# A delta-rule attention with a feed-forward layer: block 1's masks, joins and weight splits in another order

## The chip, the cores and the metric

The kernel runs on one core of one Trainium2 chip. The metric is the device time of one execution in microseconds (us). Before the change the median of three runs is 632.37 us (632.14 to 633.58).

## The reference

Inputs: q, k, v of shape (4, 8, 768, 48) (batch, heads, steps, width) and beta (4, 8, 768); weights w_in (384 x 2048) and w_out (2048 x 384), all float32. For every batch and head, one step after the other:

```
kn = k / (|k| + 1e-6);  state = 0                     (48 x 48)
for t in 768 steps:
    y[t]   = q[t] @ state
    state += beta[t] * outer(kn[t], v[t] - kn[t] @ state)
x = y as (3072 tokens, 384)
h = x @ w_in;  out = max(0.01 * h, h) @ w_out
```

## The kernel before

**Blocks.** The 768 steps are cut into 12 blocks of 64 (`nblk`). Within a block the recurrence becomes a triangular system; only its result and the state pass to the next block. Each block has a Gram product (`gram`: k with k and q), an inverse (`inv`), the attention (`solve`) and the feed-forward layer of its 256 tokens (`ffn`, 16 slices f of 128 hidden units). `gram` masks its product with the triangle on VectorE (`masked`, L320: rq), copies k's part with ScalarE (L307: gs) and the corners with VectorE (L328: gm), and writes gs through DRAM (L311: gd) into L, the system in the layout of the inverse (L341). Blocks 0 and 1 get their Gram from `first` instead (masks at L264) and are inverted together (b = 0); every later block alone. b counts the inverses: L1 and T1 belong to block 2, L2 and T2 to block 3.

**Inverse and attention.** `inv` takes the norms from L's diagonal (`norms`, L360 to L369, sixteen short steps on VectorE up to L423) and then runs 31 elimination steps (`eliminate`, L384 and L389, two interleaved chains). For a single block T is then copied by ScalarE in another layout (L449), and both layouts go through DRAM (td at L456, tt at L457). For blocks 0 and 1, `place` copies the halves of T to their places (L468). `merge_z` and `merge_u` join the halves (pz, pu; from block 2 on pz needs the transfers sq from tt and td, L516 and L519). `solve` then goes through stages kt (pk, and beta on VectorE, L623), step_w (pw), step_y (py) and step_s (pc); `columns` (px) makes x of the next block.

**The layer.** For block 0 it runs in float32, for the others as three products of high and low halves (fp32r): x is split in xh and xl, the hidden activation in gh (ScalarE, L722) and gl (VectorE, L727). The weights come in eight packed groups j of two f. Per group: load_w (a DMA), `pack` (ScalarE, L148), `conv` (four steps on VectorE, L158 to L161), `expand` (ScalarE, L168), `final` (VectorE, L175), after which block 0 can use it; `lows` then makes the halves for block 1 on (ScalarE casts the high part, L184; VectorE subtracts, L186). `pack` of group j uses the buffer of group j - 5, so packs 5, 6 and 7 wait for lows 0, 1 and 2.

**The order.** All generators are written in one program order: every block has 17 slots, slot s starts with slice s of `ffn`, then come the entries of the table `work` for that slot, then steps of `solve`, `inv` and `gram`, spread over the slots of `SV`, `IV` and `GG`. `behind(mark)` adds that an instruction isn't issued before a marked one. From this a scheduler fixes the order of each engine's queue when the kernel is built; on the chip each engine works its queue in that order. SP issues nearly all DMAs. PSUM leaves four buffers (`ps_a`) in rotation for all products but the layer's.

Of the kernel before, what the change touches and what calls it, by code (L numbers as in the profile page):

```python
# [47 lines left out]
def delta_moe_kernel(ctx: ExitStack, tc, kq0, kqT, kv, qT, beta, cst, w_all, out, nblk):  # L48
# [66 lines left out]
    wi, wo = ([{}, {}] for _ in range(2))  # L115
    raws, mark = {}, {}

    def behind(name):

        return tc.issue_after(mark[name]) if name in mark else nullcontext()  # L120

# [57 lines left out]
    def lows(j, gate):  # L179
        g = parts[j][0]  # L180
        t = sb.tile([P, 8 * DO], F32R, tag=f"w{j}", name=f"w{j}", bufs=1)
        hi, lo = t[:, 0:4 * DO], t[:, 4 * DO:]
        with behind(gate):
            nc.scalar.copy(hi, g)  # L184
# [16 lines left out]
    def first():  # L201
# [28 lines left out]
        for g in range(NGR):  # L230
            for i, y, u, (k, _) in each(g):
                l = (g * GU + u) * HC
                for e in range(2):
                    h = k[:, e * HC:(e + 1) * HC]
                    nc.tensor.matmul(diag[y][i * 64 + e * HC:i * 64 + (e + 1) * HC, l:l + HC], h, h, start=True, stop=True)
# [9 lines left out]
        for g in range(NGR):  # L245
            for i, y, u, (k, _) in each(g):
                l = (g * GU + u) * HC
                nc.tensor.matmul(low[y][corner[i], l:l + HC], k[:, HC:], k[:, 0:HC], start=True, stop=True)
# [6 lines left out]
        for g in range(NGR):  # L255
            for i, y, u, (k, q) in each(g):
                nc.tensor.matmul(bank[g][y][i * 64:(i + 1) * 64, u * C:(u + 1) * C], k, q, start=True, stop=True)
        yield
        for n in range(2):
            for g in range(NGR):  # L260
# [6 lines left out]
            after(d)  # L267
            done.add((gram, n))
# [4 lines left out]
    def gram(n):  # L273
# [16 lines left out]
        for g in range(NGR):  # L290
# [7 lines left out]
            for p in range(NPAIR):  # L298
                for c in range(2):
                    for b in range(2):  # L300
                        r = slice(b * R0, b * R0 + D)
                        with behind("ph") if n > 2 else nullcontext():
                            nc.tensor.matmul(ps[b][c * 64:(c + 1) * 64, p * 128:(p + 1) * 128],  # L303
# [70 lines left out]
    def eliminate(b, L, j, T, m):  # L374
# [4 lines left out]
        for x in range(min(m, 2)):  # L379
# [19 lines left out]
    def inv(b):
# [28 lines left out]
        for j in range(HC - 1):  # L428
# [3 lines left out]
            if j == HC - 2:  # L432
# [13 lines left out]
                else:  # L446
                    n = NB[b][0]
                    Tt = X[:, M * HC:].rearrange("p (i m) -> p i m", m=M)
                    nc.scalar.copy(Tt.rearrange("p i m -> p m i"), T)  # L449
                    td = dr.tile([2, HC, HS, HC], F32, tag="td", name=f"td{n}")  # L450
                    tt = dr.tile([HS, HC, HC], F32, tag="tt", name=f"tt{n}")
                    Tts[n] = td, tt
                    for x in range(2):
                        a = x * 64
                        for e in range(2):
                            nc.sync.dma_start(td[e, x::2].rearrange("m l i -> l m i"), T[a + e * HS:a + (e + 1) * HS])  # L456
                        nc.sync.dma_start(tt.rearrange("l i (x m) -> x l i m", m=M)[x], Tt[a:a + HS])  # L457
# [8 lines left out]
    def place(n, g, e):  # L466
        a = n * 64 + e * HC
        with behind("h" if n else "inverse"):  # L468
            return (nc.scalar.copy if e or n else nc.vector.tensor_copy)(
                half_of(n, g, e), Tts[n][0][a:a + HC].rearrange("p (y g u) i -> p g y u i", y=2, g=NGR)[:, g])  # L470
# [10 lines left out]
    def product(n, name, pairs):  # L481

        ps = ps_a.tile([P, 512], F32, tag="a", name=f"{name}{n}")
        with behind("po"):
            for q, w, lhs, rhs in pairs:
                nc.tensor.matmul(ps[q * HC:(q + 1) * HC, w * P:(w + 1) * P], lhs, rhs, start=True, stop=True)  # L486
        return ps[:, 0:2 * P]

    def merge_z(n, g, t):

        T, Tt = Tts[n]
        if n < 2:
# [34 lines left out]
    def merge_u(n, g, t):  # L527

        if n < 2:
# [32 lines left out]
    def lengths(n):  # L562
# [3 lines left out]
        nc.tensor.matmul(ps[DN, 0:HS], nrm[b][i * 64:i * 64 + 64], eye0[i * 64:i * 64 + 64], start=True, stop=True)  # L566
# [13 lines left out]

    def solve(n):
# [5 lines left out]
        nt = nts.pop(n)  # L587
# [21 lines left out]
        def kt(g):  # L609

            t, k, v = tv(n, g), of("k", n, g), of("v", n, g)
            if n:
                pv = out_of("pk", g, C)
                for c, u, r in heads(D):
                    nc.tensor.matmul(pv[r, u], k[DN, c, u], t[DN, c, u // NPAIR, u % NPAIR], start=True, stop=True)  # L615
                for c in range(2):
                    nc.scalar.mul(t[UP, c], pv[c * 64:c * 64 + D].rearrange("p (y v) t -> p y v t", y=2), -1.0)  # L617
            if not n:
                return
            for s in range(GS):  # L620
                us = slice(s * NPAIR, (s + 1) * NPAIR)
                with behind("gl"):
                    nc.vector.tensor_tensor(  # L623
                        v[DN, :, us], v[DN, :, us],
                        nt[DN, g, :, us].rearrange("p h (u o) -> p h u o", o=1).broadcast_to([C, 2, NPAIR, D]), ALU.mult)

        def step_w(g):
            t, v = tv(n, g), of("v", n, g)
            pv = out_of("pw", g, D)
            for c, u, e in quarters():  # L630
                a = c * C + e * HC
                nc.tensor.matmul(pv[a:a + HC, u], t[:, c, u // NPAIR, u % NPAIR, e * HC:(e + 1) * HC], v[:, c, u], start=True, stop=True)  # L632
# [276 lines left out]
```

## Time and profile before

| | |
|---|---|
| median of 3 runs | 632.37 us |
| profiled execution | 629.7 us, its span 627.9 us |
| TensorE (PE), its weight loads (PEld) | busy 582.0 us (93%), 533.5 us (85%) |
| VectorE (DVE) | busy 432.8 us (69%) |
| ScalarE (ACT) | busy 329.9 us (53%) |
| chain of work that ended last | PE 81%, DVE 7%, ACT 5%, DMA 3% |

The profile is of one execution. A busy share is a mean over the whole span, in which the first three blocks differ from the rest: the weights are converted there, and the first inverses run. What is read of a single block is read from its own stretch of the trace. A stretch is named by the first gh of a block; there the layer's slice 0 of that block begins.

### The profile page before, as it was taken

What the parts mean: (1) busy time and instruction counts of PE and PEld (TensorE: products, weight loads), DVE (VectorE), ACT (ScalarE), POOL (GpSimd) and SP (SyncE); (2) the same over time, 40 slices, a digit from 0 to 9 for tenths busy, and PEclk for the clock granted to TensorE, in tenths of its full rate; (3) what the DMA queues carried; (4) which work ended last, traced back from release to release, by engine and by line L of the source; (5) the groups of instructions that cost most, each with busy time, mean ns of one, the idle gap of its engine ahead of it and who ended that gap; (6) DMA issues with size and microseconds to landing.
All of it is one profiled execution on the core that took longest, in us unless ns stands there. A gap on an engine that the chain in (4) does not pass through costs nothing.

```text
span 627.9 us, 22383 instructions
## 1 busy us (share of the span) xinstructions
PE 582.0 (93%) x9122; PEld 533.5 (85%) x9122; DVE 432.8 (69%) x1949; ACT 329.9 (53%) x818; POOL 10.7 (2%) x17
## 2 busy tenths in 40 slices
PE   5278899979989989999999999999999999999996
PEld 4266677869978989999999999999999989999996
DVE  3999889979747959659659669669669569221212
ACT  3477975656535355545545545555545545544432
POOL 6000000000000000000000000000000000000000
PEclk9989999989999999999999999999999999999999
DMA  5986923361364650461560570561460540500101
GB/s 123 319 251 235 285 63 79 69 98 25 67 129 97 142 91 9 101 136 30 105 149 14 106 158 13 99 150 33 89 151 22 96 99 4 98 14 3 25 2 26
DMA packets 123431, 59.69 MB, mean 95 GB/s; under 512 B 111296, under 2 KB 114496, under 8 KB 122304
## 3 DMA queue, kind: packets, MB, share of 16 engines
q1 hardware_dynamic: 120576, 57.27, 40.0%
q10 hardware_dynamic: 2752, 0.98, 0.8%
q8 instruction: 72, 1.18, 0.8%
q14 instruction: 31, 0.25, 0.1%
HBM read 46.96 MB, written 11.27 MB: 93 GB/s over the span
## 4 chain that ended last, share of the span: by engine, by line
PE 81%; DVE 7%; ACT 5%; DMA 3%; issue 2%; SPq 1%; DVEq 0%; ACTq 0%
PE ph L719 32%; PE po L709 31%; PE pk L615 3%; PE pw L632 3%; PE py L652 3%; PE pc L642 3%; DVE T L389 2%; DVE tmp L384 2%; PE pg L303 2%; ACT gh L722 1%; PE px L687 1%; PE pu L486 1%; PE pz L486 1%; DMA kx<-in_kq 1%; DMA gd<-gs 1%
## 5 line engine op out<-in xcount | busy, mean ns | idle before, releaser
L719 PE MATMUL ph<-xh,w 128*128 128x256 f32 x1056 | 224.7, 289 | 0.0
L719 PEld LDWEIGHTS ph<-xh,w 128*128 128x128 f32 x1056 | 174.8, 189 | 7.1 <-issue 2.0
L727 DVE TENSOR_TENSOR gl<-ph,gh 128x256 fp32r<-128x256 f32 x176 | 74.4, 423 | 154.0 <-ACT ph L726 152.1
L709 PE MATMUL po<-w,gh 128*128 128x384 f32 x704 | 172.8, 343 | 5.4 <-ACT gh L722 5.4
L722 ACT ACTIVATE gh<-ph 128x256 fp32r<-128x256 f32 (+1 forms) x192 | 73.7, 384 | 158.1 <-PE ph L719 152.2
L719 PE MATMUL ph<-xl,w 128*128 128x256 f32 x528 | 149.0, 284 | 0.0
L709 PEld LDWEIGHTS po<-w,gh 128*128 128x128 f32 x704 | 121.0, 188 | 9.9 <-ACT gh L722 7.9
L389 DVE TENSOR_TENSOR T<-T,tmp 128x60 f32<-128x60 f32 (+35 forms) x661 | 111.8, 207 | 0.8
L384 DVE TENSOR_TENSOR tmp<-T,L 128x60 f32<-128x60 f32 (+35 forms) x661 | 111.2, 207 | 0.8
L709 PE MATMUL po<-w,gl 128*128 128x384 f32 x352 | 106.2, 338 | 0.0
L719 PEld LDWEIGHTS ph<-xl,w 128*128 128x128 f32 x528 | 99.9, 189 | 1.3 <-issue 0.4
L726 ACT ACTIVATE ph<-ph 128x256 f32<-128x256 f32 x176 | 67.2, 382 | 0.0
L709 PEld LDWEIGHTS po<-w,gl 128*128 128x128 f32 x352 | 61.3, 188 | 0.1
L617 ACT ACTIVATE rt<-pk 48x512 f32<-48x512 f32 x44 | 26.0, 592 | 22.4 <-PE pk L615 21.6
L320 DVE TENSOR_TENSOR rq<-pg,csb 64x256 f32<-64x256 f32 x80 | 33.9, 423 | 3.8 <-ACT gs L307 2.5
L634 ACT COPY rv<-pw 64x384 f32<-64x384 f32 x48 | 22.7, 473 | 13.4 <-PE pw L632 12.5
L644 ACT COPY rv<-pc 48x384 f32<-48x384 f32 x44 | 20.9, 475 | 11.9 <-PE pc L642 11.4
L719 PE MATMUL ph<-x,cg 128*128 128x256 f32 x96 | 24.5, 393 | 2.0 <-DVE cg L175 1.2
L719 PEld LDWEIGHTS ph<-x,cg 128*128 128x128 f32 x96 | 18.4, 197 | 7.8 <-DVE cg L175 1.6
L709 PE MATMUL po<-cg,gh 128*128 128x384 f32 x64 | 24.5, 503 | 0.0
L303 PE MATMUL pg<-kq 48*64 48x128 f32 x640 | 23.3, 274 | 0.0
L652 PEld LDWEIGHTS py<-rv,rq 128*32 128x32 f32 x1536 | 18.3, 112 | 5.5 <-ACT ph L726 2.6
(98 smaller groups left out, 584.9 us busy)
## 6 DMA issues: line engine op xcount, KB each, us to landing
wr<-in_w_all SPq DMA_DIRECT2D x8, 1536.0 KB, 13.1
kq<-in_kqT SPq DMA_DIRECT2D x40, 192.0 KB, 3.9
L<-gd SPq DMA_DIRECT2D x20, 256.0 KB, 4.0
rk<-in_kv SPq DMA_DIRECT2D x24, 192.0 KB, 3.4
rv<-in_kv SPq DMA_DIRECT2D x24, 192.0 KB, 4.1
rq<-in_qT SPq DMA_DIRECT2D x24, 192.0 KB, 3.7
out<-ob SPq DMA_DIRECT2D x46, 96.0 KB, 2.6
td<-T SPq DMA_DIRECT2D x40, 64.0 KB, 2.6
```

The source lines that it names most:

```text
L303: nc.tensor.matmul(ps[b][c * 64:(c + 1) * 64, p * 128:(p + 1) * 128], kq[r, c ^ b, p, 0], kq[r, c ^ b, p].rearrange("p x t -> p (x t)"), s ...
L320: nc.vector.tensor_tensor(qa[DN, c, b * NPAIR:(b + 1) * NPAIR], pv[b][r, 1], tri[r].rearrange("p (o t) -> p o t", o=1).broadcast_to([C, NP ...
L384: nc.vector.tensor_tensor(tv, t[:, :, j:j + 1].broadcast_to([P, k, w]), L[:, j, j + 1:].rearrange("p (o w) -> p o w", o=1).broadcast_to([P ...
L389: mark["steps"] = nc.vector.tensor_tensor(t, t, tv, ALU.subtract).ins
L617: nc.scalar.mul(t[UP, c], pv[c * 64:c * 64 + D].rearrange("p (y v) t -> p y v t", y=2), -1.0)
L634: d = nc.scalar.copy(v[DN, c], pv[c * 64:c * 64 + C])
L652: nc.tensor.matmul(pv[a:a + HC, u * D:(u + 1) * D], qa[:, c, u, e * HC:(e + 1) * HC], v[:, c, u], start=True, stop=True)
L709: i = nc.tensor.matmul(po[t][:, :DO], a[:, ts_], w, start=(f == 0 and k == 0), stop=(f == NFC - 1 and k + 1 == len(ways)))
L719: i = nc.tensor.matmul(ph, w[:, cc * P:(cc + 1) * P], a, start=(k == 0), stop=(k + 1 == len(ways)))
L722: i = nc.scalar.activation(gh, ph, AF.Prelu, alpha=0.01)
L726: i = nc.scalar.activation(ph, ph, AF.Prelu, alpha=0.01)
L727: mark["gl"] = nc.vector.tensor_tensor(gl, ph, gh.bitcast(F32), ALU.subtract).ins
```

## The change

1. The masks of block 1 go in reversed order of the two head groups, one group ahead of conv(1) and one behind final(0); conv(1) stands ahead of expand(0) and final(0).
2. `place` for block 1 uses eight DMAs on SP in place of four copies by ScalarE.
3. `lows` is split into `cast` (ScalarE) and `lows` (VectorE). The casts of groups 3 to 7 move into block 0's last slots. low(3) comes behind a mark at elimination step 20 (`el1`), lows 4 to 7 behind `el2`, which with two interleaved chains is the last step of one of them.
4. T's copy (blocks 2 to 4) goes to VectorE. td and tt leave in the order td, tt, tt, td, tied by the mark `bounce`; L of block 3 comes behind it.
5. In block 1, slots 0 to 14, `multiply` ties every TensorE instruction to the one written before it.
6. The Gram of block 4 moves from block 2 into block 1's last slots (`GG`); its gd goes by SP, before by ScalarE's queue.
7. `SV` names the slot of each step of `solve`; `IV` and `work` are new tables; the scaling by beta becomes `times` with the same instructions.

```diff
+    def multiply(*args, fn=nc.tensor.matmul, **kw):
+        with behind("pe" if fixed else None):
+            i = fn(*args, **kw)
+        mark["pe"] = i.ins
+        return i
...
-    def lows(j, gate):
+    def cast(j, gate):
...
+        with behind(gate):
+            nc.scalar.copy(t[:, 0:4 * DO], parts[j][0])
...
+    def lows(j):
...
-        with behind("dv"), behind("el2" if j > 2 else None):
+        with behind("dv"), behind("el2" if j > 3 else "el1" if j > 2 else None):
             after(nc.vector.tensor_tensor(lo, g, hi.bitcast(F32), ALU.subtract))
...
-            for g in range(NGR):
+            for g in range(NGR)[::1 - 2 * n]:
...
-                    (nc.scalar if n == GS * NGR else nc.sync).dma_start(
+                    nc.sync.dma_start(
...
-                    i = nc.sync.dma_start(Lh[b0][r * 64:(r + 1) * 64].rearrange("l j i -> l (j i)"), gd.rearrange("l j i -> l (j i)"))
+                    with behind("bounce" if n == 3 else None):
+                        i = nc.sync.dma_start(Lh[b0][r * 64:(r + 1) * 64].rearrange("l j i -> l (j i)"), gd.rearrange("l j i -> l (j i)"))
...
+        if b == 1 and j == 20:
+            mark["el1"] = mark["steps"]
...
-                    nc.scalar.copy(Tt.rearrange("p i m -> p m i"), T)
+                    (nc.vector.tensor_copy if n < 5 else nc.scalar.copy)(Tt.rearrange("p i m -> p m i"), T)
...
+                    rows(0)
                     for x in range(2):
...
+                        with behind("bounce"):
+                            d = nc.sync.dma_start(tt.rearrange("l i (x m) -> x l i m", m=M)[x], Tt[x * 64:x * 64 + HS])
+                        mark["bounce"] = d.ins
+                    rows(1)
...
+        if n:
+            for y in range(2):
+                nc.sync.dma_start(d[:, y], t[:, y])
+            return
...
+    conv(1)
     lo, hi = slice(0, 1), slice(1, 2)
     expand(0, "rv", lo)
     final(0, lo)
-    conv(1)
+    weave(1, (sv, 2, 0, 1))
+    next(gg)
+    for g in range(NGR):
+        for e in (1, 0):
+            place(1, g, e)
+    final(0, hi)
...
+    next(fg)
+    expand(1, "xh")
+    pack(3, "xh")
+    final(1)
+    conv(2)
...
-        4: ((load_w, 7, "dv"), (conv, 4), (final, 3), (lows, 0, "h0_4")),
-        5: ((expand, 4, "h0_5"), (pack, 5, "h0_4")),
-        6: ((conv, 5), (final, 4), (lows, 1, "h0_6")),
-        7: ((expand, 5, "h0_7"), (pack, 6, "h0_6")),
...
-        NF + 0: ((lows, 3, "h1_0"),), NF + 1: ((lows, 4, "h1_1"),),
-        NF + 2: ((lows, 5, "h1_2"),), NF + 3: ((lows, 6, "h1_3"),), NF + 5: ((lows, 7, "h1_5"),)}
+        4: ((pack, 5, "h0_4"), (expand, 4, "h0_4")),
+        5: ((conv, 5), (final, 4), (cast, 1, "h0_5"), (lows, 1)),
+        6: ((pack, 6, "h0_6"), (expand, 5, "h0_6")),
...
+        13: ((cast, 3, "h0_12"),), 14: ((cast, 4, "h0_13"),), 15: ((cast, 5, "h0_14"),), 16: ((cast, 6, "h0_15"), (cast, 7, "h0_15")),
+        NF + 0: ((lows, 3), (lows, 4)), NF + 2: ((lows, 5),), NF + 3: ((lows, 6),), NF + 5: ((lows, 7),)}
...
+            fixed[:] = [True] * (n == 1 and s < 15)
...
-IV, GG = ((9, 17), (6, 17), (6, 17), (2, 17)), ((2, 4), (1, 2), (1, 2))
-SV = (0, 10), (3, 13), (1, 11), (2, 12)
+IV, GG = ((7, 17), (5, 16), (3, 12), (2, 17)), ((2, 6), (1, 2), (12, 13), (16, 17))
+SV = (1, 2, 4, 5, 7, 8, 9), (7, 9, 11, 13, 14, 15), (4, 6, 7, 9, 11, 12), (3, 5, 6, 8, 10, 11)
```

What the scheduler makes of it is seen in the order of each engine's queue (line, operation, output <- inputs, partitions x elements). First VectorE where block 0 goes over into block 1 (w: lows of a group; T1, tmp1: elimination steps for block 2; gl1_0: the first gl of block 1; rq2: masks of block 3's Gram). Before:

```order
L389 TENSOR_TENSOR T1_1483<-T1_1483,tmp1_30_1_1765 128x8
L727 TENSOR_TENSOR gl1_0_1791<-ph0_72,gh1_0_1789 128x256
L384 TENSOR_TENSOR tmp1_29_0_1757<-T1_1483,L1_1072 128x16
L389 TENSOR_TENSOR T1_1483<-T1_1483,tmp1_29_0_1757 128x8x2
L384 TENSOR_TENSOR tmp1_30_0_1763<-T1_1483,L1_1072 128x8
L389 TENSOR_TENSOR T1_1483<-T1_1483,tmp1_30_0_1763 128x8
L186 TENSOR_TENSOR w3_1794<-cg3_966,w3_1794 128x1536
L727 TENSOR_TENSOR gl1_1_1808<-ph1_73,gh1_1_1806 128x256
L186 TENSOR_TENSOR w4_1811<-cg4_1022,w4_1811 128x1536
L320 TENSOR_TENSOR rq2_80<-pg3_0_0_1828,csb_74 64x256 x2
L320 TENSOR_TENSOR rq2_80<-pg3_0_1_1829,csb_74 64x256 x2
```

and now:

```order
L197 TENSOR_TENSOR w5_1703<-cg5_1136,w5_1703 128x1536
L398 TENSOR_TENSOR tmp1_29_0_1771<-T1_1359,L1_1095 128x16
L197 TENSOR_TENSOR w6_1755<-cg6_1274,w6_1755 128x1536
L197 TENSOR_TENSOR w7_1757<-cg7_1397,w7_1757 128x1536
L756 TENSOR_TENSOR gl1_0_1805<-ph0_72,gh1_0_1803 128x256
L756 TENSOR_TENSOR gl1_1_1821<-ph1_73,gh1_1_1819 128x256
L333 TENSOR_TENSOR rq2_80<-pg3_0_0_1838,csb_74 64x256 x2
L405 TENSOR_TENSOR T1_1359<-T1_1359,tmp1_29_0_1771 128x8x2
L333 TENSOR_TENSOR rq2_80<-pg3_0_1_1839,csb_74 64x256 x2
L398 TENSOR_TENSOR tmp1_30_0_1777<-T1_1359,L1_1095 128x8
L405 TENSOR_TENSOR T1_1359<-T1_1359,tmp1_30_0_1777 128x8
L465 COPY T1_1359<-T1_1359 128x16x32
```

The low of group 4 stands one row above the second fence. The lows of groups 4 to 7 now stand ahead of gl1_0; before, lows 3 to 7 came behind it, in turn with the later gl. The last steps of the elimination and T's copy now come behind gl1_1.

Second SP in block 1 (td2 and tt2: the two layouts of T for block 2; gd3 and L2: the Gram of block 3 on its way; sq0 and sq1 feed pz2; kq4: inputs of block 4's Gram). Before:

```order
L456 DMA td2_1770<-T1_1483 32x16x32 x4
L281 DMA kq4_0_2736<-in_kqT 48x1024 x2
L457 DMA tt2_1771<-T1_1483 1024x1x16 x2
L311 DMA gd3_1821<-gs3_0_1826 32x8x32 x4
L516 DMA sq0_1957<-tt2_1771 32x8x32 x4
L311 DMA gd3_1821<-gs3_1_1856 32x8x32 x4
L519 DMA sq1_1959<-td2_1770 32x8x32 x2
L341 DMA L2_1820<-gd3_1821 64x1024 x2
```

and now:

```order
L294 DMA kq4_0_2710<-in_kqT 48x1024 x2
L324 DMA gd3_1831<-gs3_0_1836 32x8x32 x4
L294 DMA kq4_1_2713<-in_kqT 48x1024 x2
L324 DMA gd3_1831<-gs3_1_1866 32x8x32 x4
L473 DMA td2_1784<-T1_1359 32x16x32 x2
L479 DMA tt2_1785<-T1_1359 1024x1x16 x2
L473 DMA td2_1784<-T1_1359 32x16x32 x2
L355 DMA L2_1830<-gd3_1831 64x1024 x2
L541 DMA sq0_2067<-tt2_1785 32x8x32 x4
```

All of gd3 now goes ahead of td2 and tt2, L2 directly behind them, and the sq behind L2.

Third ScalarE in block 0, around the copies gs2_1 of block 2's Gram (rt: copies from pu and pk, cg: pack and expand of a weight group, gh0: hidden activations). Before:

```order
L168 CAST cg4_1022<-cg4_1022 128x1536
L307 COPY gs2_1_1114<-pg2_1_0_1115 128x256
L307 COPY gs2_1_1114<-pg2_1_1_1116 128x256
L540 ACTIVATE rt0_82<-pu1_0_1165 32x2x4x32 x2
L540 ACTIVATE rt1_83<-pu1_1_1184 32x2x4x32 x2
L722 ACTIVATE gh0_6_1258<-ph0_72 128x256
L184 CAST w1_1267<-cg1_409 128x1536
```

and now:

```order
L751 ACTIVATE gh0_5_1180<-ph1_73 128x256
L190 CAST w1_1189<-cg1_409 128x1536
L751 ACTIVATE gh0_6_1270<-ph0_72 128x256
L176 CAST cg5_1136<-cg5_1136 128x1536
L156 COPY cg6_1274<-wr6_982 128x1536
L652 ACTIVATE rt0_82<-pk1_0_1192 48x2x256 x2
L652 ACTIVATE rt1_83<-pk1_1_1213 48x2x256 x2
L320 COPY gs2_1_1234<-pg2_1_0_1235 128x256
L320 COPY gs2_1_1234<-pg2_1_1_1236 128x256
```

The copies gs2_1 stood ahead of the copies from pu and of the cast of group 1; now they stand behind that cast, expand(5), pack(6) and the copies from pk.

## Rows read from the trace of the kernel before

**Rows 1.** Stretches; us, PE, PEld, DVE, ACT, POOL busy (x), PEclk, DMA share, GB/s

```profile
46.90:56.60 9.70, 7.09 (x200) 5.85 (x190) 8.87 (x16) 5.79 (x11) 0.00 (x0) 0.87 0.36 106
117.80:170.40 52.60, 49.25 (x730) 45.14 (x729) 44.21 (x195) 33.46 (x72) 0.00 (x0) 0.97 0.38 69
...
225.10:271.70 46.60, 46.30 (x730) 43.34 (x728) 33.63 (x172) 24.12 (x64) 0.00 (x0) 1.00 0.33 63
```

**Rows 2.** Waits of TensorE, 56 to 240 us: us in total, times, longest

```profile
PE pu L538 <- DVE rq L320: 2.8, 1, 2.8
PE pz L486 <- DMA sq<-tt: 2.3, 1, 2.3
```

**Rows 3.** Timeline of VectorE: start us, us, instruction, count [idle before <-releaser]

```profile
63.92 0.56 DVE L158 TENSOR_SCALAR cg<-cg 128x768 uint32<-128x768 uint32 x1 [0.76 <-ACT cg L148]
...
68.36 1.76 DVE L175 SCALAR_TENSOR_TENSOR cg<-wr,cg 128x1536 uint32<-128x1536 uint32 x1 [1.70 <-ACT cg L168]
...
71.82 1.97 DVE L623 TENSOR_TENSOR rv<-rv,nt 64x384 f32<-64x384 f32 x4
...
80.66 1.75 DVE L320 TENSOR_TENSOR rq<-pg,csb 64x256 f32<-64x256 f32 x4
82.44 0.59 DVE L328 COPY gm<-gs 32x256 f32<-32x256 f32 x2
83.06 1.76 DVE L186 TENSOR_TENSOR w<-cg,w 128x1536 fp32r<-128x1536 f32 x1
86.88 0.56 DVE L158 TENSOR_SCALAR cg<-cg 128x768 uint32<-128x768 uint32 x1 [2.06 <-ACT cg L148]
...
93.01 0.48 DVE L411 MEMSET T<- 128x512 f32 x1
...
119.22 0.42 DVE L727 TENSOR_TENSOR gl<-ph,gh 128x256 fp32r<-128x256 f32 x1
...
144.58 0.35 DVE L363 RECIPROCAL rc<-sr 128x32 f32<-128x32 f32 x1
144.96 0.22 DVE L364 SCALAR_TENSOR_TENSOR rc<-rc,L 128x32 f32<-128x32 f32 x1
...
147.22 1.29 DVE L423 TENSOR_TENSOR L<-L,cb 128x512 f32<-128x512 f32 x2
```

**Rows 4.** Timeline of ScalarE, 75 to 123 us

```profile
75.62 0.67 ACT L307 COPY gs<-pg 128x256 f32<-128x256 f32 x2
...
85.25 1.60 ACT L148 COPY cg<-wr 128x1536 bf16<-128x1536 bf16 x1
86.70 2.44 ACT L617 ACTIVATE rt<-pk 48x512 f32<-48x512 f32 x4
...
121.96 1.12 ACT L449 COPY T<-T 128x512 f32<-128x512 f32 x1
```

**Rows 5.** Timeline of SP (issue of transfers), 80 to 136 us

```profile
80.57 1.83 SPq L311 DMA_DIRECT2D gd<-gs  x4
83.85 1.10 SPq L341 DMA_DIRECT2D L<-gd  x2
...
123.69 1.37 SPq L457 DMA_DIRECT2D tt<-T  x2
...
135.07 1.13 SPq L341 DMA_DIRECT2D L<-gd  x2
```

**Rows 6.** DMA issues of the page: count, KB each, us to landing

```profile
L<-gd SPq DMA_DIRECT2D x20, 256.0 KB, 4.0
```

**Rows 7.** Timeline of TensorE in block 1, start of two f in a row

```profile
135.92 0.28 PE L719 MATMUL ph<-xh,w 128*128 128x256 f32 x1
...
138.04 0.28 PE L719 MATMUL ph<-xh,w 128*128 128x256 f32 x1
```

**Rows 8.** Stretches again, for TensorE's granted clock (PEclk)

```profile
76.80:80.20 3.40, 3.40 (x29) 2.46 (x26) 3.32 (x4) 1.25 (x4) 0.00 (x0) 0.50 0.46 125
219.00:223.00 4.00, 1.77 (x11) 1.45 (x10) 2.08 (x10) 1.99 (x5) 0.00 (x0) 1.00 0.59 130
```

More of the change, by code (lines that the diff above doesn't have):

```diff
@@ L115, in delta_moe_kernel @@
     wi, wo = ([{}, {}] for _ in range(2))
+    fixed = []
     raws, mark = {}, {}
@@ L247, in first @@
                 l = (g * GU + u) * HC
-                nc.tensor.matmul(low[y][corner[i], l:l + HC], k[:, HC:], k[:, 0:HC], start=True, stop=True)
+                multiply(low[y][corner[i], l:l + HC], k[:, HC:], k[:, 0:HC], start=True, stop=True)
             for n in range(2):
@@ L266, in first @@
                           tri[r].rearrange("p (o v t) -> p o v t", o=1, v=1).broadcast_to([C, 2, NPAIR, C]), ALU.mult)
-            after(d)
-            done.add((gram, n))
+                after(d)
+                done.add((gram, n))
+                if n:
+                    yield
             yield
@@ L452, in inv, with rows @@
                     Tts[n] = td, tt
+                    def rows(x):
+                        for e in range(2):
+                            a = x * 64 + e * HS
+                            with behind("bounce"):
+                                d = nc.sync.dma_start(td[e, x::2].rearrange("m l i -> l m i"), T[a:a + HS])
+                            mark["bounce"] = d.ins
+                    rows(0)
                     for x in range(2):
[L454 to L457, printed above, removed]
+                        with behind("bounce"):
+                            d = nc.sync.dma_start(tt.rearrange("l i (x m) -> x l i m", m=M)[x], Tt[x * 64:x * 64 + HS])
+                        mark["bounce"] = d.ins
+                    rows(1)
                 done.add((inv, b))
@@ L467, in place @@
         a = n * 64 + e * HC
-        with behind("h" if n else "inverse"):
-            return (nc.scalar.copy if e or n else nc.vector.tensor_copy)(
-                half_of(n, g, e), Tts[n][0][a:a + HC].rearrange("p (y g u) i -> p g y u i", y=2, g=NGR)[:, g])
+        d, t = half_of(n, g, e), Tts[n][0][a:a + HC].rearrange("p (y g u) i -> p g y u i", y=2, g=NGR)[:, g]
+        if n:
+            for y in range(2):
+                nc.sync.dma_start(d[:, y], t[:, y])
+            return
+        with behind("inverse"):
+            return (nc.scalar.copy if e else nc.vector.tensor_copy)(d, t)
     squares = {}
@@ L579, in lengths, with times @@
                         nc.scalar.mul(v[DN, c, u], v[DN, c, u], nt[DN, g, c, u:u + 1])
+    def times(n, g, nt):
+        v = of("v", n, g)
+        for s in range(GS):
+            us = slice(s * NPAIR, (s + 1) * NPAIR)
+            with behind("gl"):
+                nc.vector.tensor_tensor(
+                    v[DN, :, us], v[DN, :, us],
+                    nt[DN, g, :, us].rearrange("p h (u o) -> p h u o", o=1).broadcast_to([C, 2, NPAIR, D]), ALU.mult)
     def solve(n):
@@ L614, in kt @@
                 for c, u, r in heads(D):
-                    nc.tensor.matmul(pv[r, u], k[DN, c, u], t[DN, c, u // NPAIR, u % NPAIR], start=True, stop=True)
+                    multiply(pv[r, u], k[DN, c, u], t[DN, c, u // NPAIR, u % NPAIR], start=True, stop=True)
                 for c in range(2):
                     nc.scalar.mul(t[UP, c], pv[c * 64:c * 64 + D].rearrange("p (y v) t -> p y v t", y=2), -1.0)
[L618 to L625, printed above, removed]
+            if n:
+                times(n, g, nt)
         def step_w(g):
@@ L641, in step_s @@
                 with nullcontext() if n else behind("ph"):
[L642 removed]
+                    multiply(pv[r, u], k[:, c, u], v[:, c, u], start=True, stop=True)
             for c in range(2):
@@ L832, in delta_moe_kernel @@
                 fn(*args)
-            weave_at(s, n, (sv, (NS + (n == 0)) * (n + 1 < nblk), *SV[at]), (iv, NI * (n + 2 < nblk), *IV[at]),
-                     (gg, NGR * (n < 3), *GG[min(n, 2)]), (gg, NGR * (1 < n < nblk - 3), 12, 13))
+            for k in range(0 if n + 1 == nblk else SV[at].count(s)):
+                next(sv)
+            weave_at(s, n, (iv, NI * (n + 2 < nblk), *IV[at]),
+                     (gg, NGR * (n < 2), *GG[n > 0]), (gg, NGR * (0 < n < nblk - 3), *GG[2 if n > 1 else 3]))
 WEARLY, NPACK, NG = 4, 3, 5
```

64 lines of the change are left out of this document (28 added, 36 removed).

## The prediction

> **What bounds the kernel now.** I read the stretches between the first hidden activations (gh) of the blocks first [rows 1]. Block 3, from 225.1 us to 271.7, takes 46.60 us, and TensorE is busy for 46.30 of them; the later blocks repeat it. Nothing but less work on TensorE could shorten those. Block 1 takes 52.60 us, and block 2, from 170.4 to 225.1, takes 54.7. Together that is 14.1 us more than two such blocks; part of it is the second Gram product that block 2 holds. All of the change lies ahead of block 3. From there on both orders differ in little but SP's, so I leave the rest as it is. The sum asks one thing: when does block 3 start?
>
> Then the waits of TensorE [rows 2]. It waits 2.8 us for VectorE's masks at pu in block 0 and 2.3 us for a transfer at pz in block 1: these two the change attacks by name. The last view is VectorE's order of time in block 0 [rows 3]. It runs almost without a break up to gl1_0, the first gl of block 1, which ends at 119.22 + 0.42 = 119.64. Three waits are left in it: 0.76 at 63.92, 1.70 at 68.36 and 2.06 us at 86.88, all for ScalarE's packs and expands. Block 1 can't begin its second layer before gl1_0. So the wait at pu is not what sets its start: VectorE is. VectorE up to gl1_0 is the first leg of my sum, TensorE in block 1 the second, block 2 the third.
>
> **Leg 1: VectorE up to gl1_0.** Removed: the three waits, 4.52 us. conv(1) and the masks now stand where VectorE waited, and ScalarE loses the four placements that stood ahead of the expands. Added: five lows (subtractions that split the weights). Before, lows 3 to 7 stand behind gl1_0, one between each two gl, where TensorE has work beside them. Now all five stand ahead of it: 5 x 1.76 = 8.8 us [rows 3], four of them in one run just before it, as the order shows. TensorE can't send block 1's products before that, however early it is itself.
>
> One new wait stands on this leg. The second half of block 2's Gram is copied (gs2_1) behind pack(6) and four copies of pk. pack(6) writes a buffer that low(1) must have read. low(1) ended at 83.06 + 1.76 = 84.82; less the first two waits (2.46), and less beta's products, one set of masks and the corner copies, which now follow it (1.97 + 1.75 + 0.59), that is 78.05. A pack takes 1.60, the pk copies 2.44, the two gs copies 0.67 [rows 4]: gs2_1 is there at 82.8. Before, the first gd transfer was issued at 80.57, the second half of L half of 1.10 us behind 83.85 [rows 5], and L takes 4.0 to land [rows 6]: 7.8 us. So L lands at 90.6. VectorE would be there at 93.01 - 4.52 + 0.48 = 89.0 [rows 3], and waits **1.6 us**. The bounds are 0 (pack(6) in time) and 4.4 (the pk copies held for another 2.8 us, as TensorE was at pu). So gl1_0 ends at 119.64 - 4.52 + 8.8 + 1.6 = **125.5**, bounds 123.9 and 128.3.
>
> The eight transfers that now place block 1's halves of T I cost at nothing. They leave SP behind conv(1), when the DMA engines are busy for 0.36 of the time [rows 1]; eight issues at 0.46 (four take 1.83 [rows 5]) and one landing like L's make 7.7 us, and their user, pz1, stands behind block 0's first products, 9.7 us later. If that cover goes, TensorE stands at pz1, and makes it up while it waits for VectorE later. The wait at pu I cost at nothing too: TensorE gets ahead by 2.8 us and waits the longer for gl1_0.
>
> **Leg 2: block 1 from gl1_0.** TensorE's steady 46.30 us hold what is left of the block, except the first products of f1 and f2, which are done by then. One f takes 138.04 - 135.92 = 2.12 us, half of it in its first layer [rows 7]: 46.3 - 2.1 = 44.2. Block 3's Gram is done as well, block 4's comes in: one for one, no gain in this block.
>
> The waits of this leg are those that a fixed order of TensorE can't fill with other work. The L of block 3 (L2) is now issued behind all transfers of T, and these behind T's copy. What the copy costs on VectorE no row shows. The nearest row of the engine is a low, 1.76 us for 1536 elements, a third of which is 0.6; ScalarE's own copy took 1.12 [rows 4]. I take 0.7, near the low, since the engine is the same. It ends at 125.5 + 0.42 + 1.75 (masks) + 0.7 = 128.4. Behind it SP issues tt (1.37), two td (0.9) and half of L2's 1.13 [rows 5]: the last leaves at 131.2 and lands, with 4.0, at 135.2. The six norm steps in front of gl1_5 are two reciprocals at 0.35 and four steps of about 0.2 [rows 3], 1.5 in all; gl1_5 ends at 137.1. TensorE is there at 125.5 + 5 x 2.12 = 136.1: it waits 1.0. The next ten steps take 147.22 + 1.29 - 144.96, less one gl, 3.1 us [rows 3]; gl1_6 ends at 140.6 and TensorE is there at 137.1 + 2.12 = 139.2: 1.4. At the block's end solve's last step now stands in the last slots with little behind it to fill: between 0 and one f (2.1), I take 1.0. Together 3.4, less the 0.3 that a steady block has: block 2 starts at 125.5 + 44.2 + 3.1 = **172.8**. The bounds of these waits are 0 and 12 (the late L2, below). pz2 doesn't wait any longer, it stands behind f5.
>
> **The clock.** After its wait at pu TensorE ran 3.4 us, from 76.8 to 80.2, at 0.50, the lower of its two levels, 1.2 GHz; from 219 to 223, where it stood idle for 2.2 of 4 us, it kept 1.00, 2.4 GHz [rows 8]. The wait for gl1_0, some 8 us by my sum, is of the first kind. I add nothing for it: a stretch of 3.4 us at half speed costs 1.7, and up to gl1_6 TensorE has 2.4 us of waits that take it up. The Trainium skill (TensorE: Matmul & The Clock Gate, section "HAM oscillation — how this bites in real kernels") speaks against this change: there each wait for data throttles the engine anew and the next piece of work starts cold. By that rule every new wait would be paid a second time; that is the cold rival below.
>
> **Leg 3: block 2** has one Gram now and solve(3) spread as in the steady blocks: 46.60 [rows 1]. Block 3 starts at 172.8 + 46.6 = **219.4** against 225.1: 5.7 us less. The profiled execution took 629.7 us, so 624.0; the median, 632.37, stands 2.7 above it, and I forecast **626.7 us**, 0.9% less.
>
> **Rivals.** *Covered waits* (22%): pack(6), L1 and L2 come in time, and the 1.6 of leg 1 and the 3.1 of leg 2 fall away: **622.0**. For it: each is under 2 us. Against it: the queues put the users right behind their sources.
>
> *Late L2, slower* (15%): before, L2 landed at 135.07 + 0.57 + 4.0 = 139.6 [rows 5, 6], 16.5 us after T's copy had ended at 121.96 + 1.12 = 123.08 [rows 4]; I give it 6.8 here. If T's transfers hold it as long as then, gl1_5 comes 9.7 us later, and TensorE, tied to its order, has nothing else to run: **636.4**. It is slower than before by over 0.2% from an L2 landing at 142.1 on. Against it: before, the transfers of the Gram (gd3) and of sq were issued between; now gd3 goes ahead and sq behind.
>
> *Cold TensorE* (18%): the waits for gl1_0 and gl1_5 leave a stretch of 3.4 us at half speed each, and none of it is taken up: 2 x 1.7 = 3.4, **630.1**. The page's rule would make this the likeliest; the row at 219 speaks against it.
>
> That the change does not do what it says is no rival here: the lows in front of gl1_0 and T's transfers in front of L2 stand in the order itself. The forecast keeps 45%.
>
> **The numbers.** 0.2% is 1.3 us, about what a measurement of this kernel can tell from no change. Faster by more (below 631.1): the forecast, the covered waits and somewhat over half of the cold case, 0.77. Slower (above 633.6): most of the late L2, 0.12. Between: 0.11. The range, 620.0 to 634.0, takes in the covered case, with 2 us below it for one f more that TensorE may have done before gl1_0, and the cold one; it stops short of the late L2.
>
> **What would show it.** Right: gl1_0 ending between 124 and 128 with four lows in a run before it and TensorE idle for some 8 us there; no wait at pu in block 0 and none at pz2; VectorE idle once near 89, before the norms of block 2, and once at 132 to 136; block 2 at 46 to 47 us. Wrong: gl1_0 before 122 (the lows cost less than I say) or after 130; TensorE standing at pz1; a granted clock of 0.50 behind 130; L2 landing after 140.

## The result

The changed kernel takes 639.12 us (median of 4 runs, 637.71 to 640.71) against 632.87 for the kernel before: ratio 1.010, 95% interval 1.0071 to 1.0128, 1% slower. The forecast was 626.7, 0.9% faster. The profiled execution took 640.71, the slowest of the four and 1.6 above their median, and its span is 638.9 us against 627.9.

The page shows that the chain that ended last now runs more over VectorE and the transfers (before: PE 81%, DVE 7%, DMA 3%):

```profile
span 638.9 us, 22400 instructions
PE 589.5 (92%) x9122; PEld 538.6 (84%) x9122; DVE 434.5 (68%) x1952; ACT 324.9 (51%) x811; POOL 10.7 (2%) x17
...
PE 77%; DVE 13%; DMA 4%; ACT 3%; issue 2%; SPq 1%; DVEq 0%; ACTq 0%
```

The stretches of the changed kernel, columns as in [rows 1]: block 1, block 1 from gl1_0 on, block 2, block 3:

```profile
122.20:180.10 57.90, 52.06 (x799) 48.38 (x798) 43.70 (x186) 25.71 (x70) 0.00 (x0) 0.94 0.37 66
129.30:180.10 50.80, 49.00 (x724) 45.70 (x725) 36.60 (x180) 21.94 (x60) 0.00 (x0) 0.95 0.33 56
180.10:236.20 56.10, 49.96 (x734) 46.33 (x732) 37.05 (x181) 23.25 (x63) 0.00 (x0) 0.94 0.48 89
236.20:282.60 46.40, 46.10 (x730) 43.17 (x728) 33.80 (x172) 24.19 (x65) 0.00 (x0) 1.00 0.51 103
```

Block 3 starts at 236.2, before at 225.1: all the loss lies ahead of it, as was forecast, but with the other sign. Block 1 takes 57.9 (before 52.6), block 2 56.1 (54.7). Of TensorE's waits from 110 to 240 us 12.0 us are for gl; the one at pz of [rows 2] is gone, and so is the one at pu (none of it between 50 and 110 us):

```profile
PE ph L126 <- DVE gl L756: 12.0, 4, 6.1
PE po L126 <- ACT gh L751: 3.0, 2, 2.7
```

The 2.7 us stand at 117.5, at the end of block 0, where the last gh stands in ScalarE's queue behind an instruction that waits 4.4 us for low(3) on VectorE; gl1_0, which comes later, covers them.

VectorE's timeline shows the waits of leg 1 (1.70, 1.60 and 3.02 us), the lows in front of gl1_0 (at 128.87), T's copy, and two waits for L:

```profile
55.73 1.76 DVE L183 SCALAR_TENSOR_TENSOR cg<-wr,cg 128x1536 uint32<-128x1536 uint32 x1 [1.70 <-ACT cg L176]
...
64.40 1.76 DVE L183 SCALAR_TENSOR_TENSOR cg<-wr,cg 128x1536 uint32<-128x1536 uint32 x1 [1.60 <-ACT cg L176]
...
94.93 0.19 DVE L374 TENSOR_SCALAR sr<-L 128x32 uint32<-128x32 uint32 x1 [3.02 <-DMA L<-gd]
...
122.11 3.42 DVE L197 TENSOR_TENSOR w<-cg,w 128x1536 fp32r<-128x1536 f32 x2
125.44 0.17 DVE L398 TENSOR_TENSOR tmp<-T,L 128x16 f32<-128x16 f32 x1
125.53 3.42 DVE L197 TENSOR_TENSOR w<-cg,w 128x1536 fp32r<-128x1536 f32 x2
128.87 0.75 DVE L756 TENSOR_TENSOR gl<-ph,gh 128x256 fp32r<-128x256 f32 x2
...
132.05 0.62 DVE L465 COPY T<-T 128x512 f32<-128x512 f32 x1
...
141.67 0.19 DVE L374 TENSOR_SCALAR sr<-L 128x32 uint32<-128x32 uint32 x1 [3.12 <-DMA L<-gd]
...
195.58 0.19 DVE L374 TENSOR_SCALAR sr<-L 128x32 uint32<-128x32 uint32 x1 [9.09 <-DMA L<-gd]
```

The last row is the largest: VectorE stands 9.1 us for L of block 4, and gl2_4 queues behind (the expectations below call it gl2_5; counted from gl2_0 at 180.76 it is the fifth, and TensorE waits for it until 197.0). In the kernel before, L of block 4 landed later still, 18.0 us into the block against 15.4, but there seven gl stood ahead of the norms, not four, and VectorE did not wait (SP's timeline, then VectorE's, of the kernel before):

```profile
182.55 1.14 SPq L341 DMA_DIRECT2D L<-gd  x2
```

```profile
191.17 0.12 DVE L360 TENSOR_SCALAR sr<-L 128x32 uint32<-128x32 uint32 x1
```

SP's timeline, where rows 5 had L alone, shows why L is not there by the new place of the norms. From 174.8 to 191.8 it issues almost without a break (the longest, 0.7 us, is ahead of L, for gd to land), and L comes behind sq, out, rt and its own gd:

```profile
174.78 1.78 SPq L541 DMA_DIRECT2D sq<-tt  x4
...
181.83 2.45 SPq L783 DMA_DIRECT2D out<-ob  x4
184.32 0.58 SPq L550 DMA_DIRECT2D rt<-td  x1
185.01 1.95 SPq L324 DMA_DIRECT2D gd<-gs  x4
187.00 0.45 SPq L550 DMA_DIRECT2D rt<-td  x1
187.55 1.92 SPq L324 DMA_DIRECT2D gd<-gs  x4
189.51 0.45 SPq L550 DMA_DIRECT2D rt<-td  x1
190.67 1.13 SPq L355 DMA_DIRECT2D L<-gd  x2
```

The granted clock (PEclk, the third column from the end) was 0.50 behind both of TensorE's long waits, 4.1 us at gl1_0 and 6.1 at gl2_4:

```profile
130.00:134.00 4.00, 4.00 (x18) 4.00 (x18) 3.74 (x11) 0.66 (x2) 0.00 (x0) 0.50 0.62 91
...
198.00:202.00 4.00, 4.00 (x30) 3.15 (x29) 3.87 (x19) 2.14 (x7) 0.00 (x0) 0.50 1.08 172
```

### The profile page after: what moved, and what is told of

It reads as the page before. It is cut to its first block, busy times and chain, and to the rows that moved or that the text cites. A ratio compares the mean times of both kernels' runs of the same rounds, so it can differ in the third digit from the quotient of the medians.

```text
span 638.9 us, 22400 instructions
## 1 busy us (share of the span) xinstructions
PE 589.5 (92%) x9122; PEld 538.6 (84%) x9122; DVE 434.5 (68%) x1952; ACT 324.9 (51%) x811; POOL 10.7 (2%) x17
## 4 chain that ended last, share of the span: by engine, by line
PE 77%; DVE 13%; DMA 4%; ACT 3%; issue 2%; SPq 1%; DVEq 0%; ACTq 0%
PE ph L126 31%; PE po L126 28%; PE pk L126 3%; PE pw L126 3%; DVE T L405 3%; DVE tmp L398 3%; PE pg L126 3%; PE py L126 3%; PE pc L126 2%; DMA L<-gd 2%; DVE w L197 2%; PE pu L126 1%; PE px L126 1%; PE pz L126 1%; DMA kx<-in_kq 1%
## 5 line engine op out<-in xcount | busy, mean ns | idle before, releaser
L126 PE MATMUL ph<-xh,w 128*128 128x256 f32 x1056 | 227.2, 291 | 12.0 <-DVE gl L756 12.0
L126 PEld LDWEIGHTS ph<-xh,w 128*128 128x128 f32 x1056 | 176.7, 191 | 20.0 <-DVE gl L756 13.3
L126 PE MATMUL po<-w,gl 128*128 128x384 f32 x352 | 107.6, 339 | 0.0
L126 PE MATMUL ph<-x,cg 128*128 128x256 f32 x96 | 26.9, 423 | 2.0 <-ACT gh L751 1.6
L612 DVE TENSOR_TENSOR rv<-rv,nt 64x384 f32<-64x384 f32 x44 | 22.4, 555 | 0.6
```

The costliest lines, as they stand in the source:

```text
L126: i = fn(*args, **kw)
L612: nc.vector.tensor_tensor(v[DN, :, us], v[DN, :, us], nt[DN, g, :, us].rearrange("p h (u o) -> p h u o", o=1).broadcast_to([C, 2, NPAIR, D ...
```

## The experiments

All ratios are to the kernel before on the same chip, run in turn with it.

**gd of block 4 by ScalarE** (one part undone):

```diff
-                    nc.sync.dma_start(
+                    (nc.scalar if n == GS * NGR else nc.sync).dma_start(
```

> The changed kernel with the eight gd transfers of block 4's Gram in ScalarE's queue again. In the changed kernel SP issues without a break from 174.8 to 191.8 us, these eight (3.9 us) stand ahead of L of block 4, L lands at 195.5, VectorE has waited 9.1 us for it and TensorE 6.1 behind gl2_5. Theory A (SP's queue makes L late, and that is most of the loss): L lands about 3.9 us earlier, block 2 shrinks from 56.1 to about 52, time some 4 us less than the changed kernel, near 635 on the scale where before is 632.4. Rival B (the lows in front of gl1_0 and the head are the loss, block 2's wait is for something else): block 2 stays at 56, time near 639.

Ratio 1.0123 (1.0078 to 1.0168): no gain, but not by rival B. Block 2 fell to 49.2 us, and block 1 grew by 4.6. On VectorE four gl stand ahead of the norms as in the changed kernel, and L lands 8.1 us into the block: no engine waits for it, though the block itself began 4.0 us later. So L coming behind its user was what held block 2. ScalarE's timeline shows the price: the transfers stand in its queue, the next copies wait 6.95 us, and gh2_0 and TensorE (5.99 us at 184.5) behind them.

```profile
176.22 0.37 ACT L320 COPY gs<-pg 128x256 f32<-128x256 f32 x1 [1.69 <-PE pg L126]
180.19 3.24 ACTq L324 DMA_DIRECT2D gd<-gs  x4
183.55 0.65 ACT L320 COPY gs<-pg 128x256 f32<-128x256 f32 x2 [6.95 <-DMA gd<-gs]
```

What held the issues were landings of SP's transfers: the first goes at 180.19, right behind the landing of an sq at 180.11, and the fourth behind that of an out (the chain of work, 174 to 190 us). The gd need no data of theirs; why they are tied to them stays open.

```profile
180.88 2.21 DMA out<-ob
...
183.12 0.31 ACTq L324
```

**Block 4's inverse later** (`IV`: (3, 12) to (6, 17)):

> The changed kernel with the inverse of block 4 at slots 6 to 17 of block 2, as before, not 3 to 12. Its norm steps then stand behind gl2_6 and no longer in front of gl2_5, 4 us later. Theory A (it is the place of the norm steps ahead of gl2_5, with L not there yet, that stops TensorE): TensorE's wait of 6.1 us goes down to 2 or none and with it the half-clock stretch behind it, block 2 takes 47 to 50 us and the time is 630 to 633. Rival (the later inverse is late for block 3 in turn): block 2 near 48 but block 3 longer than 46.3 by 3 or more. Rival B (loss lies in block 0 and 1): block 2 hardly shorter, 637 or more.

1.0108 (1.0061 to 1.0155). TensorE's wait at gl2_4 is gone, yet block 2 still takes 53.3 us and block 3 47.9. In its place TensorE waits 2.1 us at pw, from 200.6 on, and its clock is low behind that (0.62 and 0.53 from 202 to 210, 0.94 over the block). In the profiles block 4 starts 3.1 us earlier, not 6 to 9, and the median shows no gain: theory A has the wait right and the time wrong.

**Lows behind the gl** (mark gl0 is set by each gl):

```diff
-        with behind("dv"), behind("el2" if j > 3 else "el1" if j > 2 else None):
+        with behind("dv"), behind("gl0" if j > 3 else "el1" if j > 2 else None):
```

> The changed kernel with lows 4 to 7 behind gl1_0, gl1_2, gl1_3 and gl1_5. Theory B (four lows in one run, 6.9 us, are in front of gl1_0 and of all of block 1): gl1_0 ends near 122.4 in place of 129.3, TensorE doesn't stand idle there and its half-clock stretch goes, block 2 begins 6 to 8 us earlier, time near 632. Rival (TensorE's fixed order meets the next wait, for L of block 3 behind T's transfers): gl1_0 is 7 us earlier but block 2 begins at most 3 us earlier, time 636 or more. Block 2 itself stays at 56 in both.

0.9957 (0.9935 to 0.9978): 1.4% less than the changed kernel, the largest effect of one part. gl1_0 starts at 122.33, 6.5 us earlier, block 2 6.8 us earlier and at full clock up to there; the rival falls. Block 2, too, shrinks, to 52.3 us, which I had not expected: SP's order came out other there, and L leaves 7.6 us after the block's start, not 10.6.

```profile
121.60:173.30 51.70, 49.93 (x799) 46.06 (x798) 43.72 (x186) 25.67 (x69) 0.00 (x0) 1.00 0.43 77
173.30:225.60 52.30, 49.17 (x735) 45.73 (x733) 37.03 (x181) 23.37 (x63) 0.00 (x0) 0.97 0.49 97
```

**Block 4's Gram back in block 2** (`GG` and its streams as before, gd by ScalarE):

> The changed kernel with block 4's Gram in slots 1 and 2 of block 2 again (its gd in ScalarE's queue, as before); the inverse of block 4 stays at slots 3 to 12. Theory A' (the Gram came early enough, only its way through SP is late): L of block 4 lands later than in the changed kernel or at the same time, block 2 stays at 55 or more. Rival (moving the Gram is itself the loss): block 2 falls to about 49, time near 632.

1.005 (1.0028 to 1.0073), better than the changed kernel by 0.5%. Block 2 takes 53.5 us with 2 us more work in it: between both expectations. L lands later (196.9, 17 us into the block), but VectorE waits only 2.7 us for it. Moving the Gram was no gain by itself. The edit takes gd off SP as well, so it does not part the two. The profile is of the slowest of the ten executions, 637.61 against a median of 634.40.

**Place by ScalarE** (the four copies of before):

> The changed kernel with block 1's halves of T placed by four copies of ScalarE again, not by eight transfers. In the changed kernel these eight take SP from 45.2 to 51.3 us, the weights of group 4 leave behind them at 52.7, ScalarE waits 0.8 us for them at 60.5, and VectorE waits 1.7 us at 54.0 and 1.6 at 62.8, both for expands. Theory C (the transfers make the weights late, and that makes the waits): the two waits of VectorE fall to 1.5 us together or less, gl1_0 ends 1.5 to 2.5 us earlier, ratio to before near 1.007 (the changed kernel: 1.010). Rival (the waits come from conv(1) ahead and from TensorE's half clock in the head): both waits stay above 1 us, and ScalarE's copies add up to 2.4 us, ratio 1.010 to 1.013.

1.0114 (1.0075 to 1.0153). The two waits of VectorE fall from 3.3 to 1.5 us and gl1_0 starts 1.2 us earlier, at 127.6, but the time does not fall, and theory C is not shown. Three runs that keep the eight transfers, with the orders of VectorE, ScalarE and SP as in the changed kernel up to gl1_0 (the gd by ScalarE, by GpSimd, the inverse later), have 2.2 to 2.7 us in these waits and start gl1_0 at 127.7 to 128.3. And the weights of group 4 leave no earlier without the transfers: at 52.70 with them, 0.1 us after VectorE freed their buffer, and at 53.48 without (SP's timelines of the changed kernel, then of this one):

```profile
45.18 6.14 SPq L495 DMA_DIRECT2D rt<-tc  x8
...
52.70 1.20 SPq L141 DMA_DIRECT2D wr<-in_w_all  x2
```

```profile
53.48 0.82 SPq L141 DMA_DIRECT2D wr<-in_w_all  x2
```

What theory C describes can happen: in the profile with block 4's Gram back, of the same order up to there, SP came to the transfers at 48.03, the weights left at 56.41, 3.2 us after their buffer was free, and VectorE waited 5.46 us at 68.4.

**Lows behind, block 4's inverse at slots 5 to 14:**

> The kernel with the lows behind gl1_0 (ratio 0.996), with the inverse of block 4 at slots 5 to 14 in place of 3 to 12. There VectorE waits 6.2 us for L of block 4 at 179.8 and TensorE 2.1 behind it, and the clock is low after that. Theory A: with the norms two slots later L is there, no wait of TensorE in block 2 over 1 us and no half-clock stretch at 184 to 192; block 2 falls from 52.3 to 48 or 49, ratio 0.990. Rival (block 2 is bound by something else, or the inverse is then late for block 3): ratio 0.995 or more.

0.9966 (0.9937 to 0.9995): the rival. Block 2 51.5 us; six gl now stand ahead of the norms, and a wait of 2.1 us for pz's transfer came in place of the one for L.

**Lows behind, TensorE's order free** (`fixed[:] = []`):

> The kernel with the lows behind gl1_0 (ratio 0.996), without the fixed order of TensorE in block 1. If the fixed order makes TensorE wait where other work stood ready (rival D), its waits of 1.0, 0.8 us in block 1 go and block 1 is 1 to 3 us shorter, ratio 0.992 to 0.994. If the order is harmless (theory), the same within 0.2%: 0.994 to 0.998. If it was a gain, block 1 is longer by 2 us or more: 0.999 and up.

0.9928 (0.9904 to 0.9952): block 1 takes 50.3 us against 51.7, block 2 50.9 against 52.3. The fixed order may cost some 0.3%, but the intervals overlap and the two runs are of two chips: not shown.

**Lows behind, block 2's Gram at slots 2 to 4** (`GG`):

> The kernel with the lows behind gl1_0 (ratio 0.996), with block 2's Gram at slots 2 to 4 of block 0 as before, not 2 to 6: the second copies gs2_1 then stand ahead of pack(6) and pk. There VectorE waits 3.0 us for L of block 2 at 91.4. Theory (that wait is on the path that sets gl1_0): L lands 6 to 9 us earlier, the wait goes, gl1_0 ends about 2.5 to 3 us earlier and so does everything after it, ratio near 0.991. Rival (other waits take its place, as the pk copies or the packs later): gl1_0 less than 1 us earlier, ratio 0.995 or more.

0.9957 (0.9934 to 0.9981). gl1_0 starts 1.9 us earlier, of which 0.9 stand already at the first gh (55.3 against 56.2), and the wait for L falls to 1.4; the median shows nothing of it. It is neither answer in full: the wait goes, as the theory says, and the ratio is the rival's.

**The changed kernel, order free:**

> The changed kernel with the lows in front of gl1_0 as they are, but without the fixed order of TensorE in block 1. If the fixed order multiplies the price of the lows (theory), TensorE does the first products and the second layer's other work meanwhile, its idle 4 us before gl1_0 shrink, block 1 is 3 us or more shorter, ratio 1.005 or less. Rival (nothing else is ready, all of block 1 waits for the gl whatever the order): as the kernel with the lows behind gained 0.3% from the free order, so here, 1.007 to 1.010.

1.0105 (1.0068 to 1.0142): the rival. The fixed order does not multiply the price of the lows.

**gd of block 4 by GpSimd** (`nc.gpsimd` for ScalarE in the first edit):

> The changed kernel with the eight gd transfers of block 4's Gram issued by GpSimd, whose queue is empty there. By ScalarE they cut block 2 from 56.1 to 49.2 us, but ScalarE stood 7 us at them and TensorE waited 6.0 us at the end of block 1 for gh2_0, so that nothing was gained. Theory A (L of block 4 is late because SP's queue is): L is issued 3 to 4 us earlier, no wait for ScalarE at the seam of block 1 to 2, block 2 at 50 to 53 us, ratio 1.003 to 1.005 (the changed kernel: 1.010). Rival (the transfers themselves are slow, by whatever queue): block 2 stays at 55 or more, ratio 1.008 and up.

1.0039 (1.0022 to 1.0057): the ratio and the seam are as theory A says. L leaves 8.5 us into block 2, not 10.6, block 2 takes 48.4 us at full clock, 7.7 less; block 3 gives 1.6 back with a wait for sq. But the edit changed a second order: the scheduler put the norms two gl later on VectorE, behind gl2_5, where the changed kernel has them behind gl2_3.

```profile
178.00:226.40 48.40, 48.24 (x734) 44.55 (x732) 37.07 (x181) 23.42 (x64) 3.81 (x7) 1.00 0.55 113
226.40:274.40 48.00, 46.10 (x729) 43.22 (x728) 33.85 (x172) 24.10 (x65) 0.00 (x0) 1.00 0.43 85
```

GpSimd takes the first gd 1.0 us before the block's first gh, and VectorE's wait for L is down to 3.5 us, behind gl2_4 and gl2_5 (GpSimd's timeline, then VectorE's):

```profile
177.03 1.85 POOL L324 DMA_DIRECT2D gd<-gs  x3 [165.76 <-ACT gs L320]
```

```profile
185.59 0.42 DVE L756 TENSOR_TENSOR gl<-ph,gh 128x256 fp32r<-128x256 f32 x1 [1.17 <-ACT ph L755]
187.96 0.42 DVE L756 TENSOR_TENSOR gl<-ph,gh 128x256 fp32r<-128x256 f32 x1 [1.94 <-ACT ph L755]
191.92 0.19 DVE L374 TENSOR_SCALAR sr<-L 128x32 uint32<-128x32 uint32 x1 [3.54 <-DMA L<-gd]
```

L lands 13.8 us into the block, 1.6 earlier than in the changed kernel. With the norms behind gl2_3 that alone would have left some 4.5 of TensorE's 6.1 us, by my estimate from these two numbers. The run shows what both orders together are worth, not the queue alone.

**The kernel before with the lows in front** (casts moved, lows 3 and 4 ahead of gl1_0, 5 to 7 ahead of gl1_1):

> The kernel before with one part of the change alone: the casts of groups 3 to 7 in block 0's last slots and their five lows ahead of gl1_1 (two of them ahead of gl1_0), TensorE's order not fixed, everything else as before. Theory B (VectorE has no room there, every low ahead of the first gl costs its time): gl1_0 ends 3.5 us later, gl1_1 6 to 7 us later, block 2 begins 4 to 6 us later, ratio 1.006 to 1.010. Rival (TensorE has other work to fill, or the later gl come the faster for it): block 2 begins less than 2 us later, ratio under 1.003.

1.0045 (1.0018 to 1.0073), a loss by this part alone, smaller than expected. gl1_1 ends 6.6 us later, block 2 starts 5.0 later, but block 2 is 3.0 us shorter. That block 2 could give something back here and not in the changed kernel is my reading; no run tests it.

```profile
119.78 3.42 DVE L191 TENSOR_TENSOR w<-cg,w 128x1536 fp32r<-128x1536 f32 x2
123.21 0.42 DVE L732 TENSOR_TENSOR gl<-ph,gh 128x256 fp32r<-128x256 f32 x1
123.54 5.08 DVE L191 TENSOR_TENSOR w<-cg,w 128x1536 fp32r<-128x1536 f32 x3
128.54 0.42 DVE L732 TENSOR_TENSOR gl<-ph,gh 128x256 fp32r<-128x256 f32 x1
```

**Four edits together, in two forms**: lows behind, order free, block 2's Gram at slots 2 to 4, and for the late L either the inverse at slots 5 to 14 or gd by GpSimd:

> The changed kernel with four things taken together: the lows behind the gl, no fixed order of TensorE, block 2's Gram at slots 2 to 4 and block 4's inverse at slots 5 to 14. The kernel with the first two alone has a ratio of 0.993. Theory: the wait for L of block 2 (3.4 us of VectorE there) falls to 1.5, the one for L of block 4 to under 1 us of TensorE, so 2 to 4 us less, ratio 0.987 to 0.990. Rival (these waits are covered by others in block 1): 0.992 to 0.995.

> As the combination of four, but with block 4's inverse left at slots 3 to 12 and the gd transfers of block 4's Gram issued by GpSimd instead. Theory: both are cures for the same late L, so the ratio is the same within 0.3%, 0.986 to 0.991. If the late L costs nothing any more, both are as the kernel without either, 0.990 to 0.993.

With the later inverse 0.993 (0.991 to 0.995), 626.63 us, no better than two of the four alone. With GpSimd **0.9898 (0.9875 to 0.9921)**, 624.77 us on the same chip: faster than both kernels. It is not an earlier L that makes the difference: in both six gl stand ahead of the norms, and L lands 11.8 us into block 2 with the later inverse and 13.6 with GpSimd. What differs, besides the slots of the inverse, is what stands behind gd in SP's queue. With the later inverse TensorE waits 1.46 us at pz for an sq and 1.29 at pw; with GpSimd the sq and rt leave first, and these waits are gone or 0.2 us (SP's timelines, with the later inverse, then with GpSimd):

```profile
176.58 1.12 SPq L355 DMA_DIRECT2D L<-gd  x2
177.74 2.56 SPq L544 DMA_DIRECT2D sq<-td  x4
```

```profile
172.39 2.58 SPq L544 DMA_DIRECT2D sq<-td  x4
175.01 2.19 SPq L550 DMA_DIRECT2D rt<-td  x4
177.52 1.13 SPq L355 DMA_DIRECT2D L<-gd  x2
```

Blocks 1 and 2 with GpSimd:

```profile
119.10:169.60 50.50, 49.31 (x792) 45.83 (x791) 43.47 (x184) 25.70 (x70) 0.98 (x2) 1.00 0.44 80
169.60:217.70 48.10, 47.89 (x734) 44.52 (x732) 37.16 (x181) 23.37 (x64) 3.78 (x7) 1.00 0.54 107
```

## Why the prediction was wrong

The frame held: all that changes lies ahead of block 3, TensorE waits for gl1_0 behind the lows (4.1 us, forecast 8), the waits at pu and pz2 are gone, and later blocks are as before. Two of the signs of being wrong came: a clock of 0.50 behind 130, and L2 landing at 141.6. Block 3 was forecast at 219.4 and came at 236.2. The 16.8 us between them, leg by leg:

- **Leg 3, "block 2 has one Gram now and solve(3) spread as in the steady blocks: 46.60": +9.5, the step that failed.** I took the duration of a steady block and costed none of its waits. The change puts the Gram of block 4 at the end of block 1 and its gd on SP, among the sq, rt and out of the same seam, and the norms at slot 3. So L lands 15.4 us into the block, and the norms, four gl into it, wait for L with gl2_4 behind them. 6.1 us of TensorE's wait and 3.4 us of clock (0.06 of 56.1) make the 9.5. The wait is no accident of one execution: in the two other runs with the lows in front, gd on SP and the norms behind four gl (place by ScalarE, order free) it is 6.9 and 6.3 us, and block 2 takes 56.5 and 56.3. With L 8.1 us into the block and the same norms it is gone (gd by ScalarE), and so it is with the norms behind seven gl and a late L (inverse later). With gd on GpSimd, where L and the norms' place both change, 7.7 us of block 2 come back. The Trainium skill (DMA: Bandwidth & Descriptors, section "Issuing engines are not separate DMA queues") says that issuing from several engines saves only the sequencer's time, usually small beside the transfer. Here it is not small: eight issues of SP took 3.9 us, about as much as the 4.3 us that L takes to land. The mechanism is that of my slower rival, "Late L2", but I looked for it one block too early: L2 itself held TensorE for 1.3 us.
- **Leg 1, gl1_0 at 125.5: it ended at 129.3, +3.8.** The lows were right (five in 8.6 us, forecast 8.8). The waits were not. "Removed: the three waits" was wrong: two came back, 1.7 and 1.6 us for expands. The wait for L was 3.0, not 1.6 (gs2_1 at 85.4, not 82.8, and slower issues), inside its bounds. Together that is 4.5; 0.7 was won elsewhere, I did not trace where. How much of this is the order's and how much one execution's stays open: with the same order up to there gl1_0 ends at 128.1, 128.2, 128.7 and 132.9 in four other profiles, so 2.6 of the 3.8 stand in all five. "The eight transfers [...] I cost at nothing": they held SP from 45.2 to 51.3, 0.77 us for each and not 0.46, and I had not looked at what else waited in SP's queue. In this profile nothing did that long, since the weights of group 4 left when their buffer was free; in one of the four others they were late by it. Whether the cold head lengthened the first of the two waits for expands is not shown: it is 0.6 and 0.7 us in two of the four, 1.2 and 1.9 in the others.
- **Leg 2, 47.3 us from gl1_0 to block 2: 50.8, +3.5.** T's copy took 0.62 (forecast 0.7), the waits in all 1.8 (forecast 3.1). "I add nothing for it" on the clock was wrong: TensorE ran at 0.50, its 1.2 GHz, from 130 to 134, and 0.05 of 50.8 us, 2.5, was lost. The cold rival was right in kind: both long waits were paid a second time, though the second was not the one at gl1_5 that it named but gl2_4. The rule of the Trainium skill that I had weighed (TensorE: Matmul & The Clock Gate, "HAM oscillation — how this bites in real kernels") agrees with these rows. Besides, 46.5 us of work at full clock were left, not 44.2: the first product of f2 also waited for gl1_0 (the row of waits, ph <- gl), so only f1 was done ahead. That is worth one first layer, 1.06 us; the other 1.2 I did not trace.

The parts do not add up. The lows in front cost 0.45% alone in the kernel before, and 1.4% in the changed kernel, where block 2's late L stands behind them. That the fixed order makes this difference was tried and is not so. Whether the order of SP alone explains it stays open: in the run with the lows behind, SP's queue was another too.

## What to carry to other kernels

A step that is moved takes its transfers with it: list everything that its queue issues at the new place, and see who stands behind them, before a block is costed as "one like the steady ones". An engine without idle time ahead of a block's first user is the worst place to put work that was done in turn with that block. A wait that was bought off by moving the waiting work later came back elsewhere; taking transfers off the crowded queue paid, for all that stood behind them. And an edit to one queue can change the order of another engine: compare the orders before a run is said to test one thing.

## What the runs showed of the hardware

The head's granted clock differs between executions of the same order: in the profile of the changed kernel it came back from 0.50 near 59 us (0.51 from 53.8 to 59.2), in that of the run with gd of block 4 by GpSimd, the same up to there, near 49, with the first gh at 58.5 and 56.0. Over the 15 profiles of this case that first gh lies between 55.3 and 59.4 us. This scatter is as large as several of the effects sought, so blocks are better compared from their own start.

The length of a wait alone does not tell whether the clock falls: behind 2.0 us at 188.7 (Gram back) it was 0.59 from 190 to 194, behind 2.2 us at 221.8 (the kernel before, rows 8) it stayed at 1.00.

Transfers in ScalarE's queue cost it more than their issue: four gd, 3.24 us of issue, stood between two copies that lay 6.95 us apart, since their issues waited for landings of SP's transfers. On GpSimd the same eight took from 177.0 to 184.5, and no computing stood behind them.
